# Attention and soft mixture of experts on one core: a new order of steps, and a rearranged end

## The chip, the cores and the metric

The kernel runs on one core of a Trainium2 chip. Five engines work side by side, each with its own queue of instructions that it takes in order: TensorE (PE, matrix products), VectorE (DVE), ScalarE (ACT), GpSimd (POOL) and SyncE (SP), which here issues nearly all DMAs. PEld is TensorE's loading of the stationary operand. Results of TensorE land in PSUM, everything else lies in SBUF. The metric is the device time of one execution in microseconds.

## The reference, cut to what matters

Attention over 4 batches, 8 heads, 768 positions and 64 dimensions per head, in which a query sees the 8 global keys and the 96 keys up to itself, with a slope per head on the distance; its output, 3072 tokens of 512, goes through a soft mixture of 8 experts with 4 slots each.

```python
scores = scale * np.matmul(q, k.transpose(0, 1, 3, 2))
bias = -slopes[:, None, None] * dist[None, :, :]
scores = np.where(keep, scores + bias[None], -1e9)
a = np.exp(scores - max); a = a / (sum(a) + 1e-09)
x = (a @ v), heads side by side                # 3072 x 512
logits = x @ phi                                # 3072 x 32
d = softmax of logits over the tokens           # dispatch
slot_input = d.T @ x                            # 32 x 512
h = np.maximum(slot_input[e] @ w1[e], 0.0)      # 4 x 1024, each expert e
slot_out[e] = h @ w2[e]                         # 4 x 512
c = softmax of logits over the slots            # combine
return c @ slot_out
```

The weights w1 and w2 are 16.8 MB each in float32; they and the inputs are read once.

## The kernel before, in words

**Attention.** A unit is one batch and one pair of heads, so there are 16 units, `u` = 0 to 15. Each is cut into seven key blocks (120 local keys beside the 8 global ones) in three groups. For unit u the steps are:

- `load_qk`, `load_v`: DMAs, into two raw buffers for queries and keys and two halves of a V buffer, used by turns. So the load for unit u must wait until unit u-2 is through with that buffer.
- `scores(u,k)`, k = 0 to 2 (line 521, TensorE): products of queries and keys in one of two PSUM buffers, by turns. `biased(u,k)` (530, VectorE) adds the bias table, takes the running maximum and writes to SBUF, which frees the PSUM buffer.
- `max_t` (537, TensorE), `max_r` (542, VectorE): the maximum over partitions. `exponential(u,i)` (546, ScalarE) for each head i of the pair.
- `w_hi` (549, mostly ScalarE): a float16 copy of the weights. `w_lo(u,i,part)` (556, GpSimd or, as `w_lo_dve`, VectorE): what the copy left off, in three parts. `v_hi` (489 GpSimd or 492 ScalarE) and `v_lo` (499, VectorE): the same for V, scaled.
- `values(u,i)` (573, TensorE): 39 products of these with V, summed in the first or second bank of one PSUM tile `xx`, one bank for each head of the pair. An added column gives the sums of the weights. There is only one `xx`, so the products of unit u+1 overwrite those of unit u.
- `ev_sums`, `ev_recs` (586, 592, VectorE): sums of both heads and their reciprocals. `ev_mul(u,i)` (598, VectorE): the scaling of head i by its reciprocals, from `xx` into SBUF, with a maximum (its instruction's last part is shown as xmax).
- `tr`, `tr_copy` (610, 615/619): transposes of the scaled output. `logits` (640) with phi, and for each batch the dispatch softmax and sums (`strip_*`, `by_token*`, `dispatch*`, 672 to 738).

```python
    xx = psx.tile([P, 2, 512], F32, name="x", tag="x")
    xv = xx[0:KB, :, 0:NJ * (D + 1)].rearrange("p i (t d) -> p i t d", d=D + 1)
```

**Order.** Nothing is scheduled while it runs. One written list, `ORDER` (line 51), names all steps, and the loop at line 819 issues them in its order, each on the queue of its engine. Steps of different engines run side by side as far as data allow. A step placed behind another on the same engine starts after it. Dependences between engines are turned into waits from the order of the list: who writes or reads a tile later in the list waits for the earlier one.

**Weights.** `piece(k)` (line 356) numbers 32 pieces of 1 MB, first w1 (0 to 15), then w2 (16 to 31, where 16 to 23 serve the first 256 output columns, 24 to 31 the others). Ten buffers belong to weights alone; `free` and `extra` fill buffers of the attention stage as they come free, so 23 pieces have a place in all. Pieces 23 to 31 go over places of w1 that the first layer has used up (line 354).

**The end.** After the last dispatch (`last_dispatch`, 746), `hidden(a)` (106) for the two groups a of four experts, 64 products each and a ReLU on ScalarE; `hidden_t(a)` (120): eight transposes and two copies, so that the hidden layer can be the stationary operand; `weights_by_slot` (170): 28 transposes and eight copies, which turn the combine softmax so that slots lie on partitions, into `ct`; `check_inputs` and `set_flag` (834, 853): a test whether the inputs suit this fast path; `project(n,a)` (136): products with w2 for the column half n, 32 per group of experts, summed in bank n of `xx`; `slots_out(n)` (181, 182, VectorE): adds up high and low parts from that bank; `combine` (196 to 202): for each four token tiles the products with `ct`, copies by ScalarE and VectorE, and a DMA of 512 KB to the output.

Of the kernel before, what the change touches and what calls it, by code (L numbers as in the profile page):

```python
# [21 lines left out]
B, H, S, D = 4, 8, 768, 64  # L22
DM = H * D
NG = 8
KB = 120
P = 128
NJ = 7
# [39 lines left out]
class Moe:  # L67
# [29 lines left out]
    def hidden(self, ps, slv, w1, a, hs):  # L97


        nc = self.nc  # L100
        hp = [ps.tile([P, 512], F32, name="hp", tag="x") for _ in range(2)]
        for c in range(4):
            for n in range(2):
                for s in range(4):
                    e = 4 * a + s
                    nc.tensor.matmul(  # L106
                        out=hp[n][32 * s:32 * s + 32, :], lhsT=slv(a, c, s),
                        rhs=w1(e, c // 2)[:, (c % 2) * DF + 512 * n:(c % 2) * DF + 512 * n + 512],
                        start=(c == 0), stop=(c == 3), skip_group_check=True)
        nc.scalar.activation(out=hs[:, 0:512], in_=hp[0], func=AF.Relu)  # L110
        nc.scalar.activation(out=hs[:, 512:1024], in_=hp[1], func=AF.Relu)
# [164 lines left out]
def tile_attention_moe(ctx: ExitStack, tc: tile.TileContext, qk, v, phi, w1, w2, nn, out):  # L276
# [65 lines left out]
    for name, i, *_ in ORDER:  # L342
        if name == "free":
            held = [n for n in held if n != spaces[i][0]] + [spaces[i][0]]
    places = weights + [holders[n] for n in held]
    npl = len(places)
    extras = []
    for k, n in enumerate(held):
        at = 0
        for c0, c1 in sorted(c for h, *cs in spaces for c in cs if h == n) + [(WP, WP)]:  # L350
            if at < c0:
                extras.append((NW + k, at, c0))
            at = c1
    places += places[0:5] + places[8:8 + 27 - npl]

    def piece(k):
        m, r = divmod(k, 16)
        if m == 0:
            a, r = divmod(r, 8)
            half, s = divmod(r, 4)  # L360
        else:
            half, r = divmod(r, 8)
            a, s = divmod(r, 4)
        return m, 4 * a + s, half

    wt = {piece(k): places[k][:, 0:WP] for k in range(32)}
# [467 lines left out]
    def check_inputs():  # L834
# [12 lines left out]
        nc.vector.tensor_scalar(out=fl[:, 2:3], in0=nlo, scalar1=1.0, scalar2=None, op0=ALU.is_ge)  # L847
        nc.vector.tensor_scalar(out=fl[:, 3:4], in0=nlo, scalar1=float(WIN), scalar2=None, op0=ALU.is_le)
        nc.vector.tensor_scalar(out=fl[:, 4:5], in0=ngl, scalar1=float(NG), scalar2=None, op0=ALU.is_le)
        nc.vector.tensor_reduce(out=fl[:, 8:9], in_=fl[:, 0:8], axis=AX.X, op=ALU.min)  # L850
        nc.vector.tensor_scalar(out=fl[:, 9:10], in0=fl[:, 8:9], scalar1=-1.0, scalar2=-1.0, op0=ALU.add, op1=ALU.mult)

    def set_flag():
        ft = left.tile([P, 512], F32, name="ft", tag="x")
        nc.tensor.matmul(out=ft[0:1, 0:1], lhsT=fl[:, 9:10], rhs=ones[:, 0:1], start=True, stop=True)
        nc.vector.tensor_scalar(out=flag[0:1], in0=ft[0:1, 0:1], scalar1=0.5, scalar2=None, op0=ALU.is_ge)  # L856

    sps = [places[(5, 7)[b // 2]][0:KB, 8 * P * (b % 2):8 * P * (b % 2) + 8 * P].rearrange("p (n m) -> p n m", m=P) for b in range(B)]
    hts = [places[15][:, DF * a:DF * a + DF].rearrange("p (c m) -> p c m", c=8) for a in range(2)]
    hss = [places[6][:, DF * a:DF * a + DF] for a in range(2)]  # L860

    nc.vector.memset(fl, 1.0)
    nc.vector.tensor_reduce(out=fl[0:KB, 0:1], in_=lnat, axis=AX.XY, op=ALU.min)
    nc.vector.tensor_scalar(out=fl[0:KB, 0:1], in0=fl[0:KB, 0:1], scalar1=NEG, scalar2=None, op0=ALU.is_ge)
    moe.constants()
    moe.softmax(lnat, cst, lnat)
    for a in range(2):
        moe.hidden(left, Moe.slot_view(sl), lambda e, half: wt[0, e, half], a, hss[a])
        if a == 0:
            for b in range(B):  # L870
                moe.split(lnat[:, 8 * b:8 * b + 8], sps[b])
            for c in (0, WP // 2):
                load_w(range(npl, npl + 5), c, c + WP // 2)
        else:
            for c in range(0, WP, WP // 4):
                load_w(range(npl + 5, 32), c, c + WP // 4)
    for a in range(2):
        moe.hidden_t(left, hss[a], hts[a])
    for b in range(B):
        moe.weights_by_slot(left, sps[b], ct, [(4 * (t % 2) + t // 2, TN[t], S * b + KB * t) for t in range(NJ)])  # L880
    check_inputs()

    obs = [places[16 + i // 2][:, 4 * HF * (i % 2):4 * HF * (i % 2) + 4 * HF] for i in range(6)]
    ops = [xx[:, n] for n in range(2)]

    def project(n, a, cs=range(8)):
        moe.project(ops[n], hts[a], lambda e, h: wt[1, e, h], n, a, cs)

    def slots_out(n):
        at, w = OUT_PART[n]  # L890
        moe.slots_out(ops[n][:, 0:w], ohs[:, at:at + w], sots[:, at:at + w])

    def combine(n, t0, sizes):
# [222 lines left out]
```

## Time and profile before

| what | value |
|---|---|
| median of three runs | 214.57 us (214.01 to 214.91) |
| the profiled execution's own time | 215.71 us |
| its span, first to last instruction | 213.7 us |
| busy in the span: PE, DVE, ACT, POOL | 180.1, 148.0, 125.9, 96.8 us |
| moved by DMA | 61.38 MB, mean 287 GB/s |
| mean granted clock of TensorE | 0.971 of full |

The stages in the trace: up to about 23 us the first loads, the bias tables and the first unit's softmax; from there to about 147 us the units in turn; to 158.2 the last logits and the dispatch; to 172.1 the two hidden layers; to about 177.6 the transposes; from 177.8 to 195.9 the four projections, with part of the combine between; then the rest of the combine until 201.5 and the last output transfers.

A row of the timeline is start, duration, engine, line, operation, output <- inputs, shapes and count; in brackets stands how long the engine was idle just before and what ended that. TensorE's matrix products overlap, so a row's duration is a little longer than the distance to the next start. A row of the groups is busy time, mean ns of one, and idle time before them. A row of waits gives total, times and the longest.

### The profile page before, as it was taken

What the parts mean: (1) busy time and instruction counts of PE and PEld (TensorE: products, weight loads), DVE (VectorE), ACT (ScalarE), POOL (GpSimd) and SP (SyncE); (2) the same over time, 40 slices, a digit from 0 to 9 for tenths busy, and PEclk for the clock granted to TensorE, in tenths of its full rate; (3) what the DMA queues carried; (4) which work ended last, traced back from release to release, by engine and by line L of the source; (5) the groups of instructions that cost most, each with busy time, mean ns of one, the idle gap of its engine ahead of it and who ended that gap; (6) DMA issues with size and microseconds to landing.
All of it is one profiled execution on the core that took longest, in us unless ns stands there. A gap on an engine that the chain in (4) does not pass through costs nothing.

```text
span 213.7 us, 6390 instructions
## 1 busy us (share of the span) xinstructions
PE 180.1 (84%) x2633; PEld 129.7 (61%) x2633; DVE 148.0 (69%) x382; ACT 125.9 (59%) x158; POOL 96.8 (45%) x122
## 2 busy tenths in 40 slices
PE   8999779699999899979897699588799999798400
PEld 2455679587878678667766588465353276475400
DVE  4869878479888597987977868877667745153600
ACT  2108768579998698897795879861303462041500
POOL 7113977567987688896584858430000000000000
PEclk9999999889999999999999999999999999999965
DMA  5946696748999999965538169959999999849892
GB/s 150 412 157 228 175 356 239 267 179 243 374 398 371 418 336 356 375 223 191 176 125 315 44 229 306 405 178 407 395 405 349 408 404 386 308 154 340 288 337 85
DMA packets 20630, 61.38 MB, mean 287 GB/s; under 512 B 1904, under 2 KB 9328, under 8 KB 18928
## 3 DMA queue, kind: packets, MB, share of 16 engines
q1 hardware_dynamic: 20448, 60.89, 77.4%
q8 instruction: 22, 0.36, 0.7%
q14 instruction: 16, 0.13, 0.2%
q10 hardware_dynamic: 144, 0.00, 0.0%
HBM read 54.59 MB, written 6.29 MB: 285 GB/s over the span
## 4 chain that ended last, share of the span: by engine, by line
PE 53%; DVE 17%; DMA 13%; ACT 7%; issue 4%; DVEq 0%; ACTq 0%; SPq 0%
PE sc L521 12%; PE x L573 12%; DMA raw<-in_qk_dram 8%; PE hp L106 6%; DVE tb L530 6%; DMA raw<-in_w_dram 5%; PE x L510 4%; PE x L136 3%; DVE xn L598 3%; ACT tb L546 3%; PE wp L424 2%; ACT ph L549 2%; PE m L640 2%; PE cp L196 2%; PE m L610 2%
## 5 line engine op out<-in xcount | busy, mean ns | idle before, releaser
L556 POOL TENSOR_TENSOR ph<-tb,ph 128x432 f16<-128x432 f32 x89 | 90.2, 1043 | 40.5 <-ACT ph L549 33.8
L573 PE MATMUL x<-v,ph 128*128 128x65 f16 (+1 forms) x1248 | 43.8, 194 | 10.2 <-DVE xmax L598 9.9
L573 PEld LDWEIGHTS <-ph 128*128 128x128 f16 x1248 | 41.7, 98 | 15.4 <-issue 14.2
L521 PE MATMUL sc<-raw 64*128 64x216 f32 (+2 forms) x448 | 48.3, 349 | 3.2 <-DVE mx L530 1.7
L546 ACT ACTIVATE tb<-tb,nb 128x1296 f32<-128x1296 f32 x32 | 44.0, 1375 | 9.3 <-DVE nb L542 9.3
L549 ACT CAST ph<-tb 128x1296 f16<-128x1296 f32 x31 | 39.4, 1271 | 15.5 <-PE x L573 13.5
L521 PEld LDWEIGHTS sc<-raw 64*128 64x128 f32 x448 | 38.2, 193 | 11.5 <-issue 4.8
L598 DVE CUSTOM_DVE_ANT_1 xn<-x,rc 120x448 f32<-120x448 f32 x32 | 19.6, 622 | 6.5 <-PE x L573 5.8
L530 DVE CUSTOM_DVE_ANT_1 tb<-sc,tt,mx 128x864 f32<-128x864 f32 x16 | 17.8, 1115 | 3.8 <-PE sc L521 3.4
L499 DVE SCALAR_TENSOR_TENSOR v<-vt,v 128x896 f16<-128x896 f32 x16 | 20.3, 1266 | 0.0
L492 ACT ACTIVATE v<-vt 128x896 f16<-128x896 f32 x14 | 13.2, 946 | 7.1 <-DMA vt<-in_v_dram 7.1
L610 PE MATMUL m<-ident,xn 120*128 120x120 f32 x105 | 16.4, 276 | 0.7 <-DVE al L657 0.4
L610 PEld LDWEIGHTS m<-ident,xn 120*128 120x128 f32 x105 | 10.8, 141 | 3.7 <-issue 1.6
L136 PE MATMUL x<-wp,vt 128*32 128x256 f32 x112 | 10.9, 381 | 1.1 <-DVE flag L856 1.1
L530 DVE CUSTOM_DVE_ANT_1 tb<-sc,tt 128x864 f32<-128x864 f32 x8 | 8.4, 1054 | 4.3 <-PE sc L521 4.0
L106 PE MATMUL hp<-wp,sl 128*32 128x512 f32 x80 | 10.5, 593 | 0.0
L530 DVE CUSTOM_DVE_ANT_1 tb<-sc,xta,mx 128x864 f32<-128x864 f32 x8 | 8.9, 1116 | 1.6 <-PE sc L521 1.3
L530 DVE CUSTOM_DVE_ANT_1 tb<-sc,xtt,mx 128x864 f32<-128x864 f32 x8 | 8.9, 1113 | 0.9 <-PE sc L521 0.6
L510 PE MATMUL x<-const-bfloat16-1.0 128*1 128x512 bf16 x37 | 8.7, 379 | 0.0
L199 ACT COPY tb<-cp 128x512 f32<-128x512 f32 x4 | 2.1, 590 | 10.9 <-PE cp L196 10.9
L199 ACT COPY ph<-cp 128x512 f32<-128x512 f32 x8 | 4.3, 604 | 6.4 <-PE cp L196 5.8
L136 PEld LDWEIGHTS x<-wp,vt 128*32 128x32 f32 x112 | 5.5, 110 | 3.8 <-DVE flag L856 1.2
(197 smaller groups left out, 261.0 us busy)
## 6 DMA issues: line engine op xcount, KB each, us to landing
raw<-in_qk_dram SPq DMA_DIRECT2D x15, 832.0 KB, 5.9
wp<-in_w_dram SPq DMA_DIRECT2D x10, 1024.0 KB, 8.5
vt<-in_v_dram SPq DMA_DIRECT2D x16, 448.0 KB, 5.8
wp<-in_w_dram SPq DMA_DIRECT2D x10, 512.0 KB, 7.5
out_dram<-ph SPq DMA_DIRECT2D x8, 512.0 KB, 6.9
tb<-in_w_dram SPq DMA_DIRECT2D x3, 1024.0 KB, 7.9
wp<-in_w_dram SPq DMA_DIRECT2D x8, 256.0 KB, 6.0
raw<-in_w_dram SPq DMA_DIRECT2D x8, 256.0 KB, 5.6
```

The costliest lines, as they stand in the source:

```text
L106: nc.tensor.matmul(out=hp[n][32 * s:32 * s + 32, :], lhsT=slv(a, c, s), rhs=w1(e, c // 2)[:, (c % 2) * DF + 512 * n:(c % 2) * DF + 512 * n ...
L136: nc.tensor.matmul(out=o[32 * s:32 * s + 32, 0:w], lhsT=ht[:, c, 32 * s:32 * s + 32], rhs=w2(4 * a + s, half)[:, c0 + c * w:c0 + c * w + w ...
L499: nc.vector.scalar_tensor_tensor(out=vlo[k].rearrange("p j i d -> p (j i) d"), in0=vraw[k].rearrange("p j i d -> p (j i) d"), scalar=V_SC, ...
L510: nc.tensor.matmul(out=xx[0:1, 0], lhsT=busy_in[:, 0:1], rhs=busy_in, start=True, stop=True)
L521: nc.tensor.matmul(out=z[:, i, at:at + n], lhsT=r_[r, KCOL[j]:KCOL[j] + KR], rhs=r_[r, KW + KB * j:KW + KB * j + n], start=True, stop=True)
L530: nc.vector.tensor_tensor_reduce(out=tb(u)[:, :, BW * k:BW * k + BW], in0=sc[(3 * u + k) % 2][:, :, 0:BW], in1=table.unit(u % NP, k), scal ...
L546: nc.scalar.activation(out=t, in_=t, func=AF.Exp, bias=nbs[u], scale=T_SC)
L549: nc.scalar.copy(out=blocks(phi_[i])[:, :, 0:QW], in_=tb(u)[:, i].rearrange("p (s c) -> p s c", c=QW))
L556: (engine or nc.gpsimd).tensor_tensor(out=blocks(plo_[i])[:, c, 0:QW], in0=tb(u)[:, i].rearrange("p (s c) -> p s c", c=QW)[:, c], in1=bloc ...
L573: nc.tensor.matmul(out=x[:, (D + 1) * t:(D + 1) * t + d], lhsT=w[:, c:c + P], rhs=vv[:, j, i, 0:d], start=(z == 0), stop=(z == len(ops) - ...
L598: nc.vector.tensor_tensor_reduce(out=xnb[(u // 2) % 3][:, :, c:c + D], in0=xv[:, i, :, 0:D], in1=rcs.pop((u, i)).unsqueeze(2).to_broadcast ...
L610: nc.tensor.transpose(out=m[:, at:at + KB], in_=xnb[(u // 2) % 3][:, t, P * (p % 2):P * (p % 2) + P], identity=ident[0:KB, 0:KB])
```

## The change

First, `ORDER` is replaced by another list of the same length, 603 steps. The steps are the same apart from the engine of some: two transpose copies and one `w_hi` more go to ScalarE, three `w_lo` parts move from GpSimd to VectorE in the net, and `v_hi` of units 0 and 8 goes from GpSimd to ScalarE, that of units 11 and 15 the other way. In the new list both scalings of a unit stand ahead of the next unit's first product with V, except for unit 14; in the old one six units (2, 5, 6, 12, 13, 14) have their second scaling behind it. How far ahead scores, loads of weights and of V stand is different nearly everywhere. The two lists around units 1 and 2, and around units 9 and 10:

```diff
-('values', 1, 1), ('biased', 4, 0), ('scores', 4, 1), ('w_lo', 2, 0, 0), ('w_hi', 2, 1), ('scores', 4, 2), ('tr_copy', 0, 1),
-('ev_sums', 1), ('w_lo', 2, 0, 1), ('w_lo', 2, 1, 0), ('tr', 0, 0), ('ev_recs', 1), ('load_v', 3), ('max_r', 3), ('load_qk', 6),
-('ev_mul', 1, 0), ('exponential', 3, 0), ('v_hi_act', 3), ('biased', 4, 1), ('biased', 4, 2), ('ev_mul', 1, 1), ('values', 2, 0),
+('values', 1, 1), ('exponential', 2, 1), ('tr', 0, 1), ('load_v', 3), ('biased', 4, 0), ('w_hi', 2, 1), ('scores', 4, 1), ('max_r', 3),
+('ev_sums', 1), ('scores', 4, 2), ('ev_recs', 1), ('biased', 4, 1), ('ev_mul', 1, 1), ('load_qk', 5), ('tr', 0, 0), ('w_lo', 2, 0, 2),
+('ev_mul', 1, 0), ('piece', 2), ('scores', 5, 0), ('biased', 4, 2), ('w_lo', 2, 0, 1), ('w_lo', 2, 0, 0), ('values', 2, 0),
...
-('values', 9, 1), ('exponential', 11, 0), ('biased', 12, 0), ('v_lo', 10), ('logits_all', 7), ('tr', 8, 0), ('w_hi', 10, 1),
-('biased', 12, 1), ('tr_copy', 8, 1), ('strip_max', 7), ('load_qk', 13), ('ev_sums', 9), ('extra', 7), ('tr_copy', 8, 0), ('ev_recs', 9),
-('scores', 12, 2), ('ev_mul', 9, 0), ('w_lo', 10, 0, 0), ('ev_mul', 9, 1), ('w_lo', 10, 0, 2), ('scores', 13, 0), ('w_lo', 10, 0, 1), ('strip_exp', 7), ('w_lo', 10, 1, 1),
-('values', 10, 0),
+('values', 9, 1), ('max_t', 11), ('strip_max', 7), ('ev_sums', 9), ('ev_recs', 9), ('max_r', 11), ('exponential', 10, 1), ('ev_mul', 9, 1),
+('strip_exp', 7), ('tr', 8, 1), ('w_lo', 10, 0, 1), ('ev_mul', 9, 0), ('scores', 12, 1), ('scores', 12, 2), ('by_token', 7), ('v_hi', 11),
+('w_hi', 10, 1), ('exponential', 11, 0), ('values', 10, 0),
```

The weight pieces 0 to 9 stand, by the number of the unit whose scores are near, at 0, 3, 5, 6, 7, 7, 9, 9, 10 and 11 in the old list and at 2, 3, 5, 5, 7, 9, 10, 11, 14 and 15 in the new. The list now begins with `load_v(1)`, ahead of the first load of queries and keys; both `scores(0,0)` and `scores(0,1)` stand ahead of the first 15 warming products, and `table_pair(3)` ahead of the second `biased`. Near the end, `load_v(15)` stands behind piece 9 and the loads `free(0)` and `free(14)`.

Second, the end is rearranged:

```diff
-    def hidden(self, ps, slv, w1, a, hs):
+    def hidden(self, ps, slv, w1, a, hs, at=()):
...
+            for c1, do in at:
+                if c1 == c:
+                    do()
...
-    places += places[0:5] + places[8:8 + 27 - npl]
+    places += places[0:5] + places[9:9 + 27 - npl]
...
-    hts = [places[15][:, DF * a:DF * a + DF].rearrange("p (c m) -> p c m", c=8) for a in range(2)]
+    hts = [places[8][:, DF * a:DF * a + DF].rearrange("p (c m) -> p c m", c=8) for a in range(2)]
...
-    for a in range(2):
-        moe.hidden(left, Moe.slot_view(sl), lambda e, half: wt[0, e, half], a, hss[a])
-        if a == 0:
-            for b in range(B):
-                moe.split(lnat[:, 8 * b:8 * b + 8], sps[b])
-            for c in (0, WP // 2):
-                load_w(range(npl, npl + 5), c, c + WP // 2)
-        else:
-            for c in range(0, WP, WP // 4):
-                load_w(range(npl + 5, 32), c, c + WP // 4)
-    for a in range(2):
-        moe.hidden_t(left, hss[a], hts[a])
+    w1_of = lambda e, half: wt[0, e, half]
+    moe.hidden(left, Moe.slot_view(sl), w1_of, 0, hss[0])
     for b in range(B):
-        moe.weights_by_slot(left, sps[b], ct, [...])
-    check_inputs()
+        moe.split(lnat[:, 8 * b:8 * b + 8], sps[b])
+    for c in (0, WP // 2):
+        load_w(range(npl, npl + 5), c, c + WP // 2)
+    moe.hidden(left, Moe.slot_view(sl), w1_of, 1, hss[1], [(1, lambda: moe.hidden_t(left, hss[0], hts[0]))])
+    load_w(range(npl + 5, 32))
...
     project(0, 0)
+    moe.hidden_t(left, hss[1], hts[1])
+    check_inputs()
     project(0, 1)
     slots_out(0)
+    for b in range(B):
+        moe.weights_by_slot(left, sps[b], ct, [...])
     set_flag()
-    project(1, 0, range(3))
     combine(0, 0, (4,) * 5)
-    project(1, 0, range(3, 8))
+    project(1, 0)
     project(1, 1)
     slots_out(1)
     combine(0, 20, (4,))
```

`npl` is 23. The turning of the first group's hidden layer now comes behind the second chunk of the second group's products, into place 8, whose weights these two chunks were the last to read. The second group is turned behind the first projection. The turning of the combine weights comes behind `slots_out(0)`. The last four pieces of w2 go to places 9 to 12 instead of 8 to 11, each in one DMA instead of in four.

More of the change, by code (lines that the diff above doesn't have):

```diff
@@ L866, in tile_attention_moe @@
     moe.softmax(lnat, cst, lnat)
-    for a in range(2):
-        moe.hidden(left, Moe.slot_view(sl), lambda e, half: wt[0, e, half], a, hss[a])
-        if a == 0:
-            for b in range(B):
-                moe.split(lnat[:, 8 * b:8 * b + 8], sps[b])
-            for c in (0, WP // 2):
-                load_w(range(npl, npl + 5), c, c + WP // 2)
-        else:
-            for c in range(0, WP, WP // 4):
-                load_w(range(npl + 5, 32), c, c + WP // 4)
-    for a in range(2):
-        moe.hidden_t(left, hss[a], hts[a])
-    for b in range(B):
-        moe.weights_by_slot(left, sps[b], ct, [(4 * (t % 2) + t // 2, TN[t], S * b + KB * t) for t in range(NJ)])
-    check_inputs()
+    w1_of = lambda e, half: wt[0, e, half]
+    moe.hidden(left, Moe.slot_view(sl), w1_of, 0, hss[0])
+    for b in range(B):
+        moe.split(lnat[:, 8 * b:8 * b + 8], sps[b])
[3 more added lines that the diff above has]
+    load_w(range(npl + 5, 32))
     obs = [places[16 + i // 2][:, 4 * HF * (i % 2):4 * HF * (i % 2) + 4 * HF] for i in range(6)]
@@ L897, in tile_attention_moe @@
     project(0, 0)
+    moe.hidden_t(left, hss[1], hts[1])
+    check_inputs()
     project(0, 1)
     slots_out(0)
+    for b in range(B):
+        moe.weights_by_slot(left, sps[b], ct, [(4 * (t % 2) + t // 2, TN[t], S * b + KB * t) for t in range(NJ)])
     set_flag()
-    project(1, 0, range(3))
     combine(0, 0, (4,) * 5)
-    project(1, 0, range(3, 8))
+    project(1, 0)
     project(1, 1)
```

2 lines of the change are left out of this document (1 added, 1 removed).

## The prediction

> **What bounds the kernel now.** I read one stretch of time for the attention stage first, then who waits for whom on TensorE, then the timeline at each long wait. The stretch (its columns are length, then PE, PEld, DVE, ACT, POOL, then clock, DMA share and GB/s) and the waits (total, times, longest):
>
> ```profile
> 22.00:150.00 128.00, 111.96 (x1975) 92.86 (x1975) 103.02 (x263) 101.36 (x119) 88.67 (x88) 0.99 0.76 279
> ```
>
> ```profile
> PE x L573 <- DVE xmax L598: 9.9, 10, 1.9
> ...
> PE sc L521 <- DMA raw<-in_qk_dram: 1.5, 3, 0.9
> ```
>
> In the attention stage TensorE is busy 112.0 of 128.0 us. It is the bound, with VectorE and ScalarE close behind at 103 and 101. Of its 16.0 idle us, most of a single kind, 9.9 us in ten waits, is a product with V (line 573) that waits for a scaling (line 598). The timeline shows one of them, between units 1 and 2, and a scaling of unit 5:
>
> ```profile
> 36.61 0.62 DVE L598 CUSTOM_DVE_ANT_1 xn<-x,rc 120x448 f32<-120x448 f32 x1
> ...
> 37.16 1.11 DVE L530 CUSTOM_DVE_ANT_1 tb<-sc,tt,mx 128x864 f32<-128x864 f32 x1
> ...
> 38.45 1.12 DVE L530 CUSTOM_DVE_ANT_1 tb<-sc,tt,mx 128x864 f32<-128x864 f32 x1 [0.18 <-PE m L610]
> ...
> 39.49 0.62 DVE L598 CUSTOM_DVE_ANT_1 xn<-x,rc 120x448 f32<-120x448 f32 x1
> ...
> 40.17 1.71 PE L573 MATMUL x<-v,ph 128*128 128x65 f16 x39 [1.86 <-DVE xmax L598]
> ...
> 71.86 1.35 PE L573 MATMUL x<-v,ph 128*128 128x65 f16 x39
> ...
> 73.25 0.62 DVE L598 CUSTOM_DVE_ANT_1 xn<-x,rc 120x448 f32<-120x448 f32 x1 [2.34 <-PE x L573]
> ```
>
> The product at 40.17 writes only the first half of the two-bank tile, and that half was scaled by 37.23. It starts only when the scaling of the other half ends, at 40.11: the two halves are ordered as one. The last two rows show the reverse: a scaling written behind the next unit's first product (unit 5) starts only when that product ends, though it reads the other half.
>
> The Trainium skill, PSUM — Partial Sum Buffer, section "PSUM bank collisions raise a hardware error", asks for guarding by bank and quadrant, so a product and a scaling in different banks could overlap. By that rule early second scalings would buy nothing (a rival below); the rows at 40.17 and 73.25 disagree as this program is compiled.
>
> The timeline of the end shows the same, and the stretch beside it the weight stream:
>
> ```profile
> 184.74 0.19 PE L855 MATMUL ft<-ones,fl 128*1 128x1 f32 x2
> ...
> 185.51 0.48 DVE L182 SCALAR_TENSOR_TENSOR sots<-x,sgn,ohs 128x256 fp32r<-128x256 f32 x1
> ...
> 186.04 1.50 PE L136 MATMUL x<-wp,vt 128*32 128x256 f32 x24 [1.12 <-DVE flag L856]
> ...
> 192.25 0.39 PE L136 MATMUL x<-raw,vt 128*32 128x256 f32 x2
> ```
>
> ```profile
> 178.00:186.00 8.00, 6.93 (x130) 4.07 (x122) 2.91 (x17) 0.00 (x0) 0.00 (x0) 1.00 1.02 375
> 186.00:187.50 1.50, 1.46 (x25) 0.70 (x25) 0.04 (x1) 0.00 (x0) 0.00 (x0) 1.00 0.15 53
> ```
>
> The projection for the second column half starts at 186.04, as slots_out of the first half ends (185.99): it writes the other bank of that tile. TensorE loses 1.12 us. The weight stream fills the queue until about 186 (a share of 1.02, then 0.15), but its last pieces (in raw) are first read at 192.25, so it is covered by 6 us.
>
> **The change, part one: the order.** The multiset of steps is nearly kept. VectorE gains three w_lo parts and gives up two transpose copies and one w_hi; ScalarE gains these three; GpSimd loses three w_lo parts, about 3.1 us. What matters is the place. For each unit I add what TensorE has between the second product of unit u and the first of u+1, and what VectorE must do from ev_sums to the last scaling that stands ahead of it. The prices come from a stretch of the timeline in which TensorE never stops, from the chain of waits (by_token), and from the groups of instructions (busy us, mean ns of one):
>
> ```profile
> 126.59 1.00 PE L521 MATMUL sc<-raw 64*128 64x216 f32 x8
> 127.52 0.53 PE L610 MATMUL m<-ident,xn 120*128 120x120 f32 x3
> 127.98 1.07 PE L521 MATMUL sc<-raw 64*128 64x216 f32 x12
> 128.98 0.63 PE L610 MATMUL m<-ident,xn 120*128 120x120 f32 x4
> 129.45 1.34 PE L573 MATMUL x<-v,ph 128*128 128x65 f16 x39
> 130.76 0.32 PE L537 MATMUL m<-ident,mx 128*128 128x128 f32 x1
> 131.01 0.40 PE L640 MATMUL m<-xtt,phis 128*32 128x240 f32 x5
> ```
>
> ```profile
> 105.68 0.47 PE m L696 x4
> ```
>
> ```profile
> L556 POOL TENSOR_TENSOR ph<-tb,ph 128x432 f16<-128x432 f32 x89 | 90.2, 1043 | 40.5 <-ACT ph L549 33.8 <-PE m L719 5.7 <-DVE state L672 1.1
> ...
> L499 DVE SCALAR_TENSOR_TENSOR v<-vt,v 128x896 f16<-128x896 f32 x16 | 20.3, 1266 | 0.0
> L598 DVE CUSTOM_DVE_ANT_1 xn<-x,rc 120x448 f32<-120x448 f32 x32 | 19.6, 622 | 6.5 <-PE x L573 5.8
> L530 DVE CUSTOM_DVE_ANT_1 tb<-sc,tt,mx 128x864 f32<-128x864 f32 x16 | 17.8, 1115 | 3.8 <-PE sc L521 3.4 <-PE m L610 0.2
> ...
> L542 DVE CUSTOM_DVE_ANT_0 m<-m,shift 128x128 f32<-128x128 f32 x16 | 4.7, 292 | 1.9 <-ACT tb L546 1.7 <-PE m L537 0.2
> ...
> L592 DVE RECIPROCAL rc<-rsall 120x14 f32<-120x14 f32 x16 | 3.8, 239 | 0.3
> ...
> L586 DVE TENSOR_TENSOR rsall<-x,eps 120x14 f32<-120x14 f32 x16 | 2.7, 170 | 3.4 <-PE x L573 3.1
> ...
> L542 DVE DVE_READ_ACCUMULATOR2_ANT nb<- 128x1 f32 x16 | 2.3, 141 | 0.0
> ```
>
> From start to start, TensorE pays 0.93 for a short scores step, 0.46 and 0.47 for transposes, 1.00 for a long scores step, 1.31 for a product, 0.25 for max_t and 0.47 for by_token; VectorE pays 1.11 for biased, 1.27 for v_lo, 0.62 for a scaling, 0.24 and 0.17 for ev_recs and ev_sums, 0.43 for max_r. Unit 1 of the old order: TensorE has two scores and one transpose, 0.93 + 1.00 + 0.47 = 2.40; VectorE has 0.17 + 0.24 + 0.43 + 0.62 + 2 x 1.11 + 0.62 = 4.30. It is short by 1.90; the trace has 1.86. Unit 0 is short by 3.19 - 2.18 = 1.01. The same sum gives 0.55, 2.13, 0.96 and 0.10 behind units 8, 10, 11 and 13 and nothing elsewhere: 6.65 in all, against the 9.9 measured, so the sum misses about a third.
>
> In the new order unit 1 has three scores and two transposes, 2 x 0.93 + 1.00 + 0.46 + 0.47 = 3.79, against 0.17 + 0.24 + 1.11 + 2 x 0.62 = 2.76: nothing is short. Only unit 0 (0.08), unit 13 (1.65 against by_token, max_t and one transpose, 1.18) and unit 14 (1.03 against one transpose, 0.47) stay short, 1.11 in all. Unit 14 keeps its second scaling behind the next product. The waits thus shrink by 6.65 - 1.11 = 5.5 us, if nothing else comes last.
>
> Something else may. From one unit's second product to the next's I summed the listed steps for each engine and took the largest sum. Behind unit 9 the old order gives VectorE four biased, two v_lo and small steps, 10.3 us; the new one three biased, one v_lo and both scalings, 7.8. Over the 15 stretches the largest sums add to 121.3 before and 117.5 after, a gain of 3.8. I take the middle of the two counts, **4.6 us**. The lower bound is no gain, as the next engine has only 9 us less work than TensorE; the upper is all ten waits less the remainder, 9.9 - 1.1 = 8.8.
>
> The start is taken as zero. A V load now stands ahead of the first q/k load, and a table scaling ahead of the second biased, but both first scores precede the 15 warming products that held the second one. Each way it is below 1 us. The steps moved on SP's queue are weight pieces: two of 1 MB and some extras come before unit 6, two fall back to units 13 and 14. They hide under TensorE if q/k loads land in time (rival D). The V load of unit 15 now stands behind three weight loads; its reader comes about a unit, 7 us of TensorE's work, later, and only what its landing takes beyond that would count. The scaled V copies that change engine (units 0 and 8 to ScalarE, 11 and 15 to GpSimd) cancel.
>
> **Part two: the end.** The number of matmuls is unchanged. From the timeline of the old end:
>
> ```profile
> 172.03 1.97 PE L120 MATMUL htp<-ident,wp 128*128 128x128 f32 x16
> ...
> 173.84 3.83 PE L170 MATMUL ctp<-ident,wp 120*128 120x120 f32 x28
> ...
> 174.04 0.69 DVE L126 COPY vt<-htp 128x512 f32<-128x512 f32 x1 [0.18 <-PE htp L120]
> ```
>
> slots_out (two steps of 0.48) now runs under the 28 transposes of weights_by_slot, 3.83 us, so the 1.12 us wait goes. If that cover were gone it would cost the same 1.1 again. The first turning of the middle layer moves between chunks of the second hidden layer; its input has been ready, so it stays 1 us of TensorE. The second follows the first projection; its last copy (0.69) has only a single transpose of check_inputs beside it and could hold TensorE by some 0.5, but the next four chunks need only the earlier copy, so I take zero. The last four pieces come whole instead of in quarters, and the last must wait for the whole second hidden layer. Their reader moves from 192.25 to about 191, still 5 us behind the end of the stream. If the stream came late, each us would count in full. End: **1.1 us**, bounds 0.6 (that hold paid) and 1.1.
>
> **The sum.** The profiled execution took 215.7 us around its span of 213.7; minus 4.6 and 1.1 it would take 210.0. The runs' median is 214.57, 1.1 lower, so the forecast is 214.57 - 5.7 = **208.9 us**.
>
> **Rivals.**
>
> A, the forecast: 208.9, its own range 206.5 to 211.5, chance 0.55.
>
> B, all gets out of the way: 8.8 + 1.1, and the slow stretch behind the wait at 40.17 goes too.
>
> ```profile
> 41.00:42.00 1.00, 1.00 (x19) 0.91 (x18) 0.00 (x0) 0.06 (x1) 0.00 (x0) 0.50 1.02 422
> ```
>
> ```profile
> 41.81 2.95 PE L521 MATMUL sc<-raw 64*128 64x216 f32 x16
> ```
>
> The clock was 0.50 there; 2.95 against 0.93 + 1.00 and 1.71 against 1.34 make 1.4 us. Time 214.57 - 11.3 = 203.3. For it speaks that the count found the places; against it that VectorE and ScalarE are 80% busy. Chance 0.12. The Trainium skill, TensorE: Matmul & The Clock Gate, "What's actually happening", puts the drop behind about 3.4 us without work; here it followed 1.86 idle us, so the trace is harsher.
>
> C, another engine takes over: VectorE or ScalarE ends last at the same places, and only the end's 1.1 stays: 213.5. For it speaks that the count of largest sums leaves only 3.8, and that it needs all sums packed without a gap. Chance 0.15.
>
> D, slower: the q/k loads. A raw buffer is refilled between scores(u-2,2) and scores(u,0). TensorE's work between them falls for units 4, 5 and 6 from about 6.0, 7.7 and 6.9 to 4.3, 6.6 and 6.5 us, while more weights share the queue. The median landing of these loads, and the longest in the chain of waits:
>
> ```profile
> raw<-in_qk_dram SPq DMA_DIRECT2D x15, 832.0 KB, 5.9
> ```
>
> ```profile
> 68.69 10.03 DMA raw<-in_qk_dram
> ```
>
> At the median landing of 5.9 it costs 1.6 at unit 4, and there VectorE's three biased ahead hide most of it. With all three landing after L, the loss is 3L - 17.4; it eats the 5.7 from L = 7.7. One load took 10.03; at 8.2 the loss is 7.2, and the time 216.1. Against it: no such wait before 62 us, 1.5 us in all. Chance 0.12.
>
> E, the change doesn't do what it says: the two banks are ordered separately, and another wait is misnamed at these places. Then neither part gains: 214.6. The rows at 40.17, 73.25 and 186.04 speak against it. Chance 0.06. It is what the rule of the Trainium skill (PSUM — Partial Sum Buffer, quoted above) would give.
>
> **How the numbers follow.** A measurement of this kernel can tell about 0.5%, 1.1 us, from no change: faster is below 213.5, slower above 215.6. A and B and a little over half of C are faster, 0.75; the rest of C and most of E are no change, 0.12; D and a slip of E are slower, 0.13. The range goes from 204.0, inside B, to 214.2, behind C: it leaves out D (0.12), half of E (0.03) and two fifths of B (0.05).
>
> **What would show it.** Waits of line 573 for line 598 below 3 us in all; each second scaling directly behind its first, with no wait for a product except behind unit 14; TensorE above 93% between 22 us and the last product; no idle time ahead of the second half's projection. Wrong would be: those waits gone and the last product not earlier (C), waits of scores for raw above 4 us (D), or a wait of similar length for the weights ahead of line 136.

## The result, and the profile after

The changed kernel takes 203.78 us (median of four runs, 203.60 to 204.43) against 214.29 us for the kernel before on the same chip: a ratio of 0.956, with a 95% interval of 0.946 to 0.965. It is faster: 9.5 us by the ratio and 10.5 by the medians, where the forecast of 208.9 had 5.7. The median lies 0.2 us below the low end of the range; by the ratio the 214.57 us that the sum began from become 205.0, which is inside it. Single executions of a kernel can come out over 1.5% slower than its fastest: the ratios leave these out, and so do the times given for the experiments, but the traces of the runs at 211.23 and 212.33 us below are of such executions. The profiled execution took 204.43 us, with a span of 202.6 against 213.7.

Lines have moved by 3: the products with V are now line 576, the scaling 601, the scores 524, the projection 139. First, each kernel cut at its own events: the first product with V, the last one, the first product of the hidden layers, the end of the last projection, the end. The columns are the stretch and its length, busy time of PE, PEld, DVE, ACT and POOL, the granted clock, the DMA share and GB/s. Before:

```profile
23.20:147.00 123.80, 107.76 (x1932) 90.20 (x1931) 99.61 (x254) 100.00 (x114) 87.47 (x87) 0.99 0.75 278
147.00:158.20 11.20, 9.99 (x107) 5.87 (x107) 7.45 (x33) 3.01 (x10) 0.00 (x0) 1.00 1.00 399
158.20:195.90 37.70, 36.58 (x453) 19.56 (x452) 18.83 (x43) 11.53 (x20) 0.00 (x0) 1.00 0.92 338
195.90:213.70 17.80, 3.84 (x28) 3.43 (x28) 5.31 (x9) 3.71 (x7) 0.00 (x0) 0.75 0.75 247
```

After, with one more row for the middle of the attention stage:

```profile
25.00:136.20 111.20, 105.95 (x1931) 89.85 (x1931) 99.30 (x253) 99.67 (x115) 86.25 (x86) 0.98 0.84 304
136.20:147.80 11.60, 9.56 (x108) 5.79 (x110) 6.80 (x32) 3.58 (x11) 0.00 (x0) 1.00 1.01 416
147.80:184.90 37.10, 36.97 (x453) 19.50 (x453) 18.69 (x44) 11.57 (x20) 0.00 (x0) 1.00 0.94 358
184.90:202.60 17.70, 3.77 (x28) 3.36 (x28) 5.32 (x9) 3.72 (x7) 0.00 (x0) 0.69 0.68 223
60.00:120.00 60.00, 60.00 (x1094) 50.59 (x1092) 56.05 (x148) 58.23 (x70) 50.17 (x50) 1.00 0.79 279
```

The whole difference of 11.1 us can be read off: the start loses 1.8 (first product at 25.0 instead of 23.2), the units gain 12.6 (123.8 to 111.2), the stretch to the hidden layers loses 0.4, hidden layers and projections gain 0.6, the tail 0.1. The start's share varies: in eight traces whose list begins like the old one the first product comes at 21.7 to 23.2, in five that begin like the new one at 24.9 to 25.8, some 2.7 us later on the mean. In the units TensorE's idle time fell from 16.0 to 5.3 us, to a busy share of 95%; its busy time fell by another 1.8. Between 60 and 120 us TensorE has no idle time, although ScalarE is busy for 97% and VectorE for 93% of that time.

The waits of TensorE that answer to those quoted before:

```profile
PE sc L524 <- DMA raw<-in_qk_dram: 5.0, 2, 2.7
...
PE x L576 <- DVE xmax L601: 2.2, 3, 0.9
```

The ten waits for a scaling have become three (9.9 to 2.2 us). So of the 12.6 us of the units 7.7 are these waits, 3.1 other idle time (the longest before, 1.90 us at 137.88 for a copy of VectorE, line 619, is gone), and 1.8 busy time. Scores wait for their queries and keys for 5.0 us instead of 1.5, at two places, one at the start and one at unit 4:

```profile
7.31 3.45 PE L524 MATMUL sc<-raw 64*128 64x216 f32 x16 [2.30 <-DMA raw<-in_qk_dram]
...
34.20 1.56 PE L524 MATMUL sc<-raw 64*128 64x216 f32 x8 [2.73 <-DMA raw<-in_qk_dram]
```

### The profile page after: what moved, and what is told of

Same layout as the page of the kernel before. It is cut to its first block, busy times and chain, and to the rows that moved or that the text cites. A ratio compares the mean times of both kernels' runs of the same rounds, so it can differ in the third digit from the quotient of the medians.

```text
span 202.6 us, 6356 instructions
## 1 busy us (share of the span) xinstructions
PE 178.2 (88%) x2633; PEld 129.8 (64%) x2633; DVE 147.0 (73%) x382; ACT 127.1 (63%) x161; POOL 94.0 (46%) x119
## 4 chain that ended last, share of the span: by engine, by line
PE 78%; DVE 6%; DMA 6%; ACT 2%; issue 1%; SPq 0%; DVEq 0%; ACTq 0%
PE sc L524 21%; PE x L576 18%; PE x L139 7%; PE hp L106 7%; DMA raw<-in_qk_dram 6%; PE m L613 6%; PE x L513 4%; PE m L643 3%; PE m L722 3%; PE cp L199 2%; PE ctp L173 2%; PE m L540 1%; DVE ph L204 1%; PE ld L722 1%; DVE ph L559 1%
## 5 line engine op out<-in xcount | busy, mean ns | idle before, releaser
L559 POOL TENSOR_TENSOR ph<-tb,ph 128x432 f16<-128x432 f32 x86 | 87.4, 1046 | 38.6 <-ACT ph L552 36.8
L576 PEld LDWEIGHTS <-ph 128*128 128x128 f16 x1248 | 42.2, 99 | 6.5 <-issue 6.2
L552 ACT CAST ph<-tb 128x1296 f16<-128x1296 f32 x32 | 40.6, 1269 | 6.5 <-PE x L576 5.8
L601 DVE CUSTOM_DVE_ANT_1 xn<-x,rc 120x448 f32<-120x448 f32 x32 | 18.9, 621 | 0.5
L502 DVE SCALAR_TENSOR_TENSOR v<-vt,v 128x896 f16<-128x896 f32 x16 | 18.6, 1162 | 0.2 <-ACT v L495 0.2
L613 PEld LDWEIGHTS m<-ident,xn 120*128 120x128 f32 x105 | 10.8, 141 | 2.5 <-issue 1.3
L139 PE MATMUL x<-wp,wp 128*32 128x256 f32 x96 | 10.7, 380 | 0.0
L106 PE MATMUL hp<-wp,sl 128*32 128x512 f32 x80 | 10.5, 593 | 0.0
L139 PE MATMUL x<-tb,wp 128*32 128x256 f32 x32 | 7.2, 379 | 0.0
L559 DVE TENSOR_TENSOR ph<-tb,ph 128x432 f16<-128x432 f32 x10 | 7.0, 729 | 0.2 <-ACT ph L552 0.2
```

The source lines that it names most:

```text
L106: nc.tensor.matmul(out=hp[n][32 * s:32 * s + 32, :], lhsT=slv(a, c, s), rhs=w1(e, c // 2)[:, (c % 2) * DF + 512 * n:(c % 2) * DF + 512 * n ...
L139: nc.tensor.matmul(out=o[32 * s:32 * s + 32, 0:w], lhsT=ht[:, c, 32 * s:32 * s + 32], rhs=w2(4 * a + s, half)[:, c0 + c * w:c0 + c * w + w ...
L502: nc.vector.scalar_tensor_tensor(out=vlo[k].rearrange("p j i d -> p (j i) d"), in0=vraw[k].rearrange("p j i d -> p (j i) d"), scalar=V_SC, ...
L552: nc.scalar.copy(out=blocks(phi_[i])[:, :, 0:QW], in_=tb(u)[:, i].rearrange("p (s c) -> p s c", c=QW))
L559: (engine or nc.gpsimd).tensor_tensor(out=blocks(plo_[i])[:, c, 0:QW], in0=tb(u)[:, i].rearrange("p (s c) -> p s c", c=QW)[:, c], in1=bloc ...
L576: nc.tensor.matmul(out=x[:, (D + 1) * t:(D + 1) * t + d], lhsT=w[:, c:c + P], rhs=vv[:, j, i, 0:d], start=(z == 0), stop=(z == len(ops) - ...
```

## The experiments

Where a time is compared, the ratio is to the kernel before, timed beside it; 1% is 2.15 us.

**Order and end apart.** The first kernel has the new list and the old end, the second the old list and the new end.

```diff
-ORDER = [the list of before]
+ORDER = [the list of the changed kernel]
```

> The kernel before with the changed kernel's order of steps; its end is left as it was. Theory (the order is where the time went: the first to the last product with V took 123.80 us before and 111.10 after, the first product began 1.84 us later): about 204.3 to 205.0 us, the ten waits of a product for a scaling (9.9 us) down to about 2.2 in three. The prediction's own size of the order (4.6): 209.7. Rival (the new end carries most of it): 212 or more.

> The changed kernel's end behind the order of steps of before. Theory (the 1.1 us wait for slots_out goes, 0.6 of it comes back as a wait of project(0, 1) for the last copy of hidden_t): 0.4 to 0.7 us below the kernel before, so about 213.7. The prediction's sum had 1.1. Rival (the new end carries most of the gain): 5 us or more below.

Measured: the order alone 204.97 us, ratio 0.962 (0.958 to 0.966), a gain of 8.1 us by the ratio; the end alone 212.2 us, ratio 0.992 (0.988 to 0.996), a gain of 1.8 (0.9 to 2.7). The stretch of the units with the order alone:

```profile
25.80:135.20 109.40, 104.59 (x1931) 88.67 (x1931) 99.31 (x253) 99.61 (x115) 86.20 (x86) 1.00 0.85 309
```

The gain is the order's, and its stretch is as short as in the changed kernel. It begins late here too, at 25.8. The end alone, by its first hidden product and its last projection:

```profile
L106 PE MATMUL hp<-wp,sl x80: 592/592/617, 154.9 to 164.8; 128*32 128x512 f32 x80
```

```profile
L139 PE MATMUL x<-raw,wp x32: 379/379/379, 188.3 to 191.6; 128*32 128x256 f32 x32
```

That is 36.7 us. The same two events in the profile of before:

```profile
L106 PE MATMUL hp<-wp,sl x80: 592/592/617, 158.2 to 168.1; 128*32 128x512 f32 x80
```

```profile
L136 PE MATMUL x<-raw,vt x32: 379/379/379, 192.3 to 195.5; 128*32 128x256 f32 x32
```

37.3 us: the trace accounts for 0.6 of the end's gain, as in the changed kernel; the interval of the ratio is too wide to say more. The expectation puts 0.6 us of what was lost down to the copy; the last experiment comes back to that.

**One kind of move out of the 603 steps.** The old list, in which only the second scaling of each unit is moved directly behind the first:

```diff
-('ev_mul', 1, 0), ('exponential', 3, 0), ('v_hi_act', 3), ('biased', 4, 1), ('biased', 4, 2), ('ev_mul', 1, 1), ('values', 2, 0),
+('ev_mul', 1, 0), ('ev_mul', 1, 1), ('exponential', 3, 0), ('v_hi_act', 3), ('biased', 4, 1), ('biased', 4, 2), ('values', 2, 0),
```

> The kernel before with one kind of move in its order: the second scaling of each unit stands directly behind the first on VectorE; nothing else is moved. Theory (a product with V waits for both scalings, so what stands between them is paid by TensorE): by the prediction's count of fill against chain the short sum falls from 6.65 us to 1.0, and the 9.9 us of waits to 1 to 3; what is pushed back (biased, v_lo) may give some of it back, so 3 to 8 us below the kernel before, 206 to 211. Rival (only the whole new order of all engines does it): within 2 us of the kernel before.

Measured: 200.84 us, ratio 0.944 (0.937 to 0.950), a gain of 12.1 us by the ratio: below the expected range, and below the changed kernel's time. The stretch of the units, and what is left of the waits:

```profile
21.70:132.20 110.50, 104.62 (x1931) 88.49 (x1930) 99.67 (x254) 99.47 (x114) 86.66 (x87) 1.00 0.83 306
```

```profile
PE x L573 <- DVE xmax L598: 2.7, 5, 1.0
```

Nothing else of the new list is needed for what it gains in the units: 110.5 us against 111.2. What the new list does differently from here is to begin some 3 us later.

**The cause itself.** The kernel before with `xx` as two tiles; its list stays:

```diff
-    xx = psx.tile([P, 2, 512], F32, name="x", tag="x")
+    xx = [psx.tile([P, 512], F32, name=f"x{i}", tag=f"x{i}") for i in range(2)]
...
-        nc.vector.tensor_tensor(out=rsall[:, 2 * u:2 * u + 2, :], in0=xv[:, :, :, D], ...)
+        for i in range(2):
+            ev_sum(u, i)
```

> The kernel before, its order and end unchanged, with the PSUM tile xx of two banks made two tiles of one bank each; the joint addition ev_sums becomes two of its kind (0.17 us each, 16 more on VectorE). Theory (the dependence goes by the tile, so a product into bank 0 waits for the scaling that reads bank 1): now a product waits only for the scaling of its own bank, the waits of the values line fall below 4 us, and the time to 206 to 211. Rival (the order goes by bank already, and the waits were for the scaling of the same bank): the waits stay near 10 us and the time within 1 us of before, or slower by up to 2.7 (16 x 0.17) with the second additions on the path.

Measured: 198.36 us, ratio 0.929 (0.924 to 0.935), well below the expected 206 to 211 and the fastest kernel of this study. Waits and timeline (PE is the first product of unit 1, DVE the second scaling of unit 0):

```profile
PE x L573 <- DVE xmax L599: 0.8, 2, 0.5
```

```profile
28.75 1.34 PE L573 MATMUL x<-v,ph 128*128 128x65 f16 x39
29.20 0.62 DVE L599 CUSTOM_DVE_ANT_1 xn<-x,rc 120x448 f32<-120x448 f32 x1
```

The product into one bank and the scaling from the other now run at the same time. So it was the tile, not the chip, that ordered them. The Trainium skill, PSUM — Partial Sum Buffer, "PSUM bank collisions raise a hardware error", asks for a guard by bank and quadrant; with a tile for each bank that guard is all that is left, and these two rows agree with it. The old end gains from it as well, because `slots_out(0)` and `project(1, 0)` now use different tiles, and the wait of 1.1 us ahead of line 136 is gone:

```profile
L106 PE MATMUL hp<-wp,sl x80: 592/592/617, 142.3 to 152.2; 128*32 128x512 f32 x80
```

```profile
L136 PE MATMUL x<-raw,vt x32: 379/379/379, 175.1 to 178.3; 128*32 128x256 f32 x32
```

36.0 us, 1.3 less than before: more than the new end gained.

**Are these two gains or one?** The two tiles and the moved scalings together, and the two tiles in the changed kernel:

```diff
+xx as two tiles, in the old list with its second scalings behind the first
```

> The kernel before with both edits that helped it alone: xx as two PSUM tiles of one bank each, and the second scaling of each unit directly behind the first. Theory (both take away one and the same wait): no more than the better of them, 197 to 200. Rival (two separate gains of 16 and 14 us): below 195.

```diff
+xx as two tiles, in the changed kernel
```

> The changed kernel with xx as two PSUM tiles of one bank each, order and end unchanged. Theory (the tile is the cause, and the new order has already taken away what it costs but for 2.2 us at units 13 to 15): 201 to 203. Rival (the two tiles speed up the chain of VectorE in every order, and so add to the new order as they did to the old one): 190 to 198.

Measured: 199.43 us, ratio 0.932 (0.924 to 0.940), and 203.45 us, ratio 0.950 (0.942 to 0.957). Neither adds to the better of its parts: the first is no faster than the two tiles alone (0.929), the second a little above the expected 201 to 203 and no clear gain over the changed kernel (0.956). It is one and the same wait, taken away in either of two ways.

The second kernel shows more: with two tiles the new list is slower than the old one, by 4.4 us by the ratios (0.950 and 0.929); the new end, which it has as well, changes nothing by itself there, as the last experiment shows. Its first product comes at 24.9 instead of 22.1, its units take 111.0 us instead of 108.8 (first product with V to the start of the last), and its scores still wait at the start and at unit 4:

```profile
PE sc L524 <- DMA raw<-in_qk_dram: 5.2, 2, 2.8
PE x L576 <- ACT ph L552: 1.4, 1, 1.4
```

The same waits for queries and keys are 0.9 us with the two tiles and the old list. The new list pays only as long as the two banks share a tile. At units 14 and 15, where the changed kernel waited 2.2 us for scalings, 0.8 of them are left, but 1.4 for a copy of ScalarE stand beside them.

**Back again, in the new list.** Behind each first scaling stand again as many VectorE steps as in the old list:

```diff
-('ev_mul', 4, 1), ('load_qk', 8), ('ev_mul', 4, 0), ...
+('ev_mul', 4, 1), ('load_qk', 8), ..., (one more step of VectorE), ('ev_mul', 4, 0), ...
```

In units 1, 2, 4, 5 and 10 the moved scaling, that of the first head, comes behind the next unit's product, and so scales that unit's values instead of its own unit's; instructions and their number are the same.

> The changed kernel with one kind of move in its order: behind the first scaling of each unit stand again as many VectorE steps ahead of the second as in the order of before (at most up to the unit's transposes or the next unit's second product). Theory (where the second scaling stands carries the gain in the new order too): the prediction's count of fill against chain rises from 1.11 to 3.42 us, six second scalings stand behind the next unit's first product again, and the time rises by 4 to 9 us over the changed kernel's 203.8, to 208 to 213. Rival (in the new order the longer fills cover it): 203 to 205.5.

Measured: 211.23 us, ratio 0.985 (0.977 to 0.993), some 7 us above the changed kernel by the medians and 6.3 by the ratios, as expected. The waits:

```profile
DVE xn L601 <- PE x L576: 6.8, 5, 2.5
...
PE x L576 <- DVE xmax L601: 6.3, 6, 2.0
```

The place of the second scaling carries the gain in the new list too; its longer fills don't cover it.

**Where the count went short.** The move of the third experiment, in two parts: only in units 0, 1, 4, 8, 10 and 11, whose second scaling stood ahead of the next product, or only in 2, 5, 6, 12, 13 and 14, where it stood behind. (In the first kernel the list changes at units 3 and 9 too, but there no VectorE step stood between the two.)

```diff
 units 0, 1, 4, 8, 10, 11 (first kernel); units 2, 5, 6, 12, 13, 14 (second kernel):
-('ev_mul', u, i), (other steps), ('ev_mul', u, 1 - i)
+('ev_mul', u, i), ('ev_mul', u, 1 - i), (other steps)
```

> The kernel before, the second scaling moved directly behind the first only in the units whose second scaling stands ahead of the next unit's first product (0, 1, 4, 8, 10, 11). By the prediction's count these hold 6.3 of the 6.65 us, so about 208.3. Theory now (the count is right for these and gives zero to the units whose second scaling stands behind the next product, where VectorE waits 5.8 us for products): 206.5 to 209.5, and the rest of the 13.8 us that all units gave lies in the others. Rival (these units carry nearly all): 200 to 203.

> The kernel before, the second scaling moved directly behind the first only in the units whose second scaling stands behind the next unit's first product (2, 5, 6, 12, 13, 14). By the prediction's count nothing is gained here (the sum rises from 6.65 to 7.27 us): 214.6 to 215.2. Theory now (these scalings hold VectorE for 5.8 us, and with it the work queued behind, which the count gave no price): 3 to 7 us below the kernel before, 207.5 to 211.5.

Measured: 204.69 us, ratio 0.955 (0.948 to 0.962), a gain of 9.7 by the ratio; and 212.33 us, ratio 0.993 (0.987 to 1.000), a gain of 1.4. The first is faster than its theory, the second slower: I had put too much on the units behind. The waits of the first:

```profile
DVE xn L598 <- PE x L573: 5.5, 4, 2.7
...
PE x L573 <- DVE xmax L598: 1.8, 4, 0.7
```

and of the second:

```profile
PE x L573 <- DVE xmax L598: 9.7, 9, 1.9
```

The waits of the kernel before that the first kernel's units held, beside the 1.86 us at 40.17:

```profile
31.98 1.33 PE L573 MATMUL x<-v,ph 128*128 128x65 f16 x39 [1.06 <-DVE xmax L598]
...
95.97 1.33 PE L573 MATMUL x<-v,ph 128*128 128x65 f16 x39 [1.09 <-DVE xmax L598]
...
113.67 1.33 PE L573 MATMUL x<-v,ph 128*128 128x65 f16 x39 [1.89 <-DVE xmax L598]
...
122.62 1.33 PE L573 MATMUL x<-v,ph 128*128 128x65 f16 x39 [1.68 <-DVE xmax L598]
```

They are 7.6 of the 9.9 us, behind units 0, 1, 8, 10 and 11; behind unit 4 nothing waited. Of the rest, 0.9 lie behind units 7 and 9, whose scalings already stood together on VectorE, and 1.5 behind 13 and 14. The prediction's count gave these five units 6.55 us: right at unit 0 (1.01) and unit 1 (1.90), a little high at 10 (2.13), about half at 8 and 11 (0.55 and 0.96). The move gave 9.7, more than the count, and more than the 8.1 us of waits that went (9.9 to 1.8). In its trace the stretch of the units is shorter by 10.8 us (113.0 against 123.8), of which 8.8 are idle time of TensorE and 2.0 busy time. The other units were worth little by themselves, although VectorE waits 5.5 us there. They give some 2.4 us (0.955 to 0.944, intervals that overlap a little) once the first ones are gone.

**The start.** In the changed kernel, the V load of unit 1 is moved:

```diff
-ORDER = [('load_v', 1), ('load_qk0', 0), ('load_phis', 0), ('load_qk', 0), ..., ('load_qk', 1), ...
+ORDER = [('load_qk0', 0), ('load_phis', 0), ('load_qk', 0), ..., ('load_qk', 1), ('load_v', 1), ...
```

> The changed kernel with one step moved: the load of V for unit 1 is issued behind the q/k loads of units 0 and 1 instead of ahead of them all. Theory (the first scores of the changed kernel wait 2.30 us for q/k because that V load shares the DMA engines with it): the wait goes and the first product with V starts 1 to 2 us earlier than 25.0, the time falls by as much against the changed kernel's 203.8, to 201.8 to 202.8. Rival (the start is set by the 15 filler matmuls of 3.42 us that now stand between the second and the third scores of unit 0): the wait goes, but the first product comes within 0.5 us of where it was, 203.3 or more.

Measured: 201.09 us, ratio 0.939 (0.932 to 0.946), 2.7 us below the changed kernel, a little more than the theory had. The first scores and all products with V:

```profile
5.51 1.00 PE L524 MATMUL sc<-raw 64*128 64x216 f32 x8
6.74 1.00 PE L524 MATMUL sc<-raw 64*128 64x216 f32 x8 [0.22 <-DMA raw<-in_qk_dram]
```

```profile
L576 PE MATMUL x<-v,ph x1248: 189/193/262, 22.0 to 134.4; 128*128 128x65 f16 x119, 128*128 128x64 f16 x60
```

The first product begins at 22.0 instead of 25.0. One load of 448 KB ahead of the queries and keys cost the start all of that, and the 15 warming products are not what sets it.

**Unit 4.** In the changed kernel, two loads are moved away from the queries and keys of unit 4:

```diff
-('load_qk', 4), ('w_lo', 1, 1, 2), ('v_hi_act', 2), ('extra', 2), ('scores', 4, 0), ... ('load_v', 3), ... ('load_qk', 5),
+('load_qk', 4), ('w_lo', 1, 1, 2), ('v_hi_act', 2), ('scores', 4, 0), ... ('load_qk', 5), ('load_v', 3), ('extra', 2),
```

> The changed kernel with two loads moved: the 192 KB piece extra(2) and V for unit 3 are issued behind the q/k load of unit 5 instead of ahead of the scores of unit 4. Theory (they share the DMA engines with the q/k load of unit 4, for which TensorE waits 2.73 us at 34.2): the wait falls below 1 us and the clock of the stretch 30 to 40 us comes back, 1 to 3 us below the changed kernel, 200.8 to 202.8. Rival (another load is then late, V for unit 3 before its products first): 203.3 or more.

Measured: 204.24 us, ratio 0.955 (0.949 to 0.962): no gain. The same place:

```profile
34.40 1.00 PE L524 MATMUL sc<-raw 64*128 64x216 f32 x8 [2.15 <-DVE mx L533]
```

```profile
34.20 0.08 DVE L533 DVE_READ_ACCUMULATOR2_ANT mx<- 128x1 f32 x1
```

The scores of unit 4 now wait for VectorE instead: the last `biased` of unit 3 frees their PSUM buffer at 34.28. The two limits lay close together, and counted from the first product (25.0 and 25.6) taking one away moved these scores by 0.4 us, from 9.2 to 8.8.

**The best parts together.** The two tiles, the old list and the new end, in which the turn of the second hidden layer now stands between chunks of the first projection:

```diff
-    project(0, 0)
+    project(0, 0, range(4))
     moe.hidden_t(left, hss[1], hts[1])
+    project(0, 0, range(4, 8))
     check_inputs()
```

> The order of steps of before, with xx as two PSUM tiles of one bank each, and the changed kernel's end, in which the turn of the second hidden layer stands behind chunks 0 to 3 of project(0, 0) instead of behind all eight. Theory (the two tiles take the waits away without any new order, the end adds its 1.1 us when the last copy of the turn is covered by four more chunks): 0.8 to 1.8 us below the 198.4 of the two tiles alone, 196.6 to 197.6. Rival (the copy's hold of 0.6 stays wherever the turn stands): 197.8 to 198.4.

Measured: 198.63 us, ratio 0.929 (0.924 to 0.934), the same as with the two tiles alone, without the gain that the theory had. The end takes 36.7 us again:

```profile
L106 PE MATMUL hp<-wp,sl x80: 592/592/617, 142.9 to 152.8; 128*32 128x512 f32 x80
```

```profile
L139 PE MATMUL x<-raw,wp x32: 379/379/379, 176.3 to 179.6; 128*32 128x256 f32 x32
```

In the changed kernel `project(0, 1)` begins as the copy on ScalarE ends (167.52), and the transpose of `check_inputs` (line 846) runs within that wait:

```profile
166.23 1.10 PE L123 MATMUL htp<-ident,wp 128*128 128x128 f32 x8
166.93 0.59 ACT L127 COPY wp<-htp 128x512 f32<-128x512 f32 x1 [3.39 <-PE htp L123]
...
167.16 0.27 PE L846 MATMUL xt<-ident,xmax 120*32 120x120 f32 x1
...
167.58 0.40 PE L139 MATMUL x<-wp,wp 128*32 128x256 f32 x1
```

Here the copy (160.34 to 160.93) is over long before:

```profile
160.34 0.59 ACT L127 COPY wp<-htp 128x512 f32<-128x512 f32 x1 [1.66 <-PE htp L123]
...
162.53 0.28 PE L847 MATMUL xt<-ident,xmax 120*32 120x120 f32 x1
...
162.76 0.40 PE L139 MATMUL x<-wp,wp 128*32 128x256 f32 x1
```

The same step in the kernel before:

```profile
177.60 0.28 PE L843 MATMUL xt<-ident,xmax 120*32 120x120 f32 x1
...
177.80 0.40 PE L136 MATMUL x<-tb,vt 128*32 128x256 f32 x1
```

From the start of that transpose to the projection pass 0.4 us in the changed kernel and 0.2 in the other two. So the copy holds TensorE by some 0.2 us, not by the 0.6 that the expectation gave it, and without that hold the end is no shorter. The rest is spread over small gaps where the new end cuts a stream of products for transposes: from the start of the last product to that of the first transpose pass 0.31 us (165.92 to 166.23) where products follow each other every 0.21. The gaps were not tested one by one.

## Why the prediction was right or wrong, point by point

- **The bound and the cause: right.** The two banks of `xx` were ordered as one. Moving the second scalings alone gives a ratio of 0.944, splitting the tile alone 0.929, both together no more (0.932). Rival E (banks ordered separately) is out.
- **The order, 4.6 us: right in mechanism, mis-sized.** The units gained 12.6 us in the trace, of which the start took back 1.8; the order alone gave 8.1 (7.3 to 9.0). The failing step is the middle of two counts. The count of fill against chain named units 0, 1, 8, 10 and 11 rightly, as the parts of the third experiment show, and for the new list units 13 and 14 (1.11 counted, 2.2 measured in three waits). But it gave 6.55 where those five units held 7.6, next to nothing for units 7, 9, 13 and 14 (0.10 against 2.4), and so missed about a third, as the prediction had noted. The measured waits were the better price, and still too low: the move that took 8.1 us of waits away gave 9.7. The upper bound of 8.8 was therefore no bound for the units, because other idle time and busy time went with the waits.
- **Partly luck.** The units gave 8.0 us more than their term, and the start took 1.8 to 2.7 that the sum had at nothing. These two errors have opposite signs, and that is why the time came as near to the forecast as it did.
- **"Something else may" (the largest sums, 3.8; rival C): wrong.** VectorE and ScalarE did not come last: at 93% and 97% of a stretch of 60 us they leave TensorE no idle time. A sum for each stretch between two products forbids work to be carried from one stretch to the next; the buffers allow it.
- **Rival B, 203.3: the time that came, though not by its sum.** Its 8.8 for the order was too little for the units (12.6), it had nothing for the start, and the dip of the clock that it counted as saved came back at another place (below).
- **The start, taken as zero with less than 1 us each way: wrong.** 1.8 us in the trace, some 2.7 on the mean of all traces, and 2.7 by the experiment that undoes it. The step that failed looked at TensorE's order (scores ahead of the warming products), not at what the V load does to the loads behind it.
- **The end, 1.1 with bounds 0.6 and 1.1: the lower bound came, 0.6.** The wait for `slots_out` is gone, but the step that gave the lower bound was wrong: the hold by the last copy, put at 0.5, takes only some 0.2 us, and the rest goes in gaps where streams of products are cut, which the sum did not have.
- **Rival D: its wait came at unit 4 (2.73 us), its price didn't.** The sentence that VectorE's three `biased` hide most of it is what the experiment shows: with the loads moved away, 2.15 us of the wait stay, for VectorE. Units 5 and 6 waited for nothing. The other 2.30 us of waits for `raw` are the start's. With 5.0 us in all, the prediction's own sign for D (above 4 us) appeared, and the time fell all the same: the sign did not tell the gain from the loss.
- **The pieces of weights, the load of V for unit 15 and the whole-piece loads at the end, at zero:** no product with V and no projection of the changed kernel waits for a DMA.

## What to carry to other kernels

A tile that spans several banks is one object for the dependences: give each independently used bank its own tile before reordering anything around it. Price a removed wait by its measured length, which here came out a little below the gain, and let a count of work name the places. Count a load that is moved ahead of others in the same queue by what it does to those behind it, at the start above all, where nothing covers it. When a wait is taken away, look for the second limit that lies just behind it.

## What was not expected of the hardware

The idle time of 2.73 us ahead of unit 4 was again followed by a low clock. The stretches of the changed kernel behind it:

```profile
34.20:35.70 1.50, 1.50 (x9) 0.98 (x10) 0.58 (x1) 0.00 (x0) 0.00 (x0) 0.60 0.99 377
35.70:37.00 1.30, 1.30 (x26) 1.30 (x26) 1.07 (x2) 0.00 (x0) 0.00 (x0) 0.50 1.02 416
37.00:38.00 1.00, 1.00 (x21) 0.99 (x19) 0.00 (x0) 0.00 (x0) 0.00 (x0) 0.54 1.02 431
```

The granted clock was 0.50 to 0.60 for nearly 4 us. With the 1.86 us of the kernel before, that makes two idle times followed by about half the clock. Both are below the 3.4 us that the Trainium skill names (TensorE: Matmul & The Clock Gate, "What's actually happening"). But the same length doesn't always do it: behind the 1.89 us at 113.67 of the kernel before the clock stayed at 1.00, and so it did between 30 and 40 us in the kernel with the new order alone, where the scores wait up to 1.9 us:

```profile
114.00:116.00 2.00, 2.00 (x45) 1.78 (x41) 1.08 (x2) 0.92 (x1) 0.00 (x0) 1.00 0.96 399
```

What decides it is not shown by these traces. In the units the same products and scores were busy for 107.8 us before, 105.9 after, and 104.6 with the scalings moved alone, at a clock of 0.99, 0.98 and 1.00. Busy time goes down as the stalls go. How much of that is the clock and how much the restarting of a broken stream was not told apart.
